# One VectorE tile fewer in a split-softmax attention kernel, with the order planned for a shorter ScalarE wave

## The chip, the cores and the metric

The kernel runs on one core of a Trainium2 chip. The metric is the device time of one execution in microseconds (us), the median of several runs; each profiled execution also has a span, some 2 us shorter, from its first to its last instruction. Every run carries a state; only fast runs are compared. The engines are PE (TensorE matmul; PEld is its weight load), ACT (ScalarE), DVE (VectorE), POOL (GpSimd) and SP, which here only issues transfers (SPq in the trace).

## The reference

```python
B, H, S, D = 1, 32, 2048, 640     # Dh = 20
qn = q / (sqrt((q * q).sum(-1, keepdims=True)) + eps)
kn = k / (sqrt((k * k).sum(-1, keepdims=True)) + eps)
logits = einsum('bhqd,bhkd->bhqk', qn, kn) * t[None, :, None, None]
attn = softmax(logits, axis=-1)
return einsum('bhqk,bhkd->bhqd', attn, v)
```

There are 32 heads of 2048 x 2048 logits with only 20 channels, so the exponentials are the work: 134 million of them.

## The kernel before

Each head's keys form 16 row blocks. For each block and each of four groups of 512 queries TensorE writes one unit (128 x 512) of logits to PSUM. Then one of two engines does the exponential. ScalarE takes waves of 2 and 3 units in turn, from PSUM tile psA to p_ring:

```python
act[w] = add("ACT", f"exp{w}", lambda e, tk: e.activation(
    p_ring[...], psA[...], ACT.Exp), 0.0633 + n / 1200.0, qks + war, w)
```

VectorE takes tiles of 4 units. It turns a logit into the bits of an fp16 power of two (two pieces per tile, psD to xt) and makes three shifted copies (ss), whose weighted sum with xt corrects the approximation. For some tiles the third copy is made by GpSimd instead:

```python
e.tensor_scalar(xt[...], psD[...], X_MUL, X_ADD, ALU.mult, ALU.add)   # VectorE, 2 per tile
e.tensor_scalar(dst, x, float(PHASES[i]), None, ALU.add)              # VectorE, 2 or 3 per tile
e.tensor_tensor(dst..bitcast(I32), xt..bitcast(I32), two, ALU.add)    # GpSimd, the third of some tiles
```

How many of the 16 blocks of each head go to VectorE is the list DVE_TILES; for how many of these GpSimd makes the third copy is KDN. Everything is written as tasks with a planned duration. A planner in the kernel's own source simulates the engines, picks an order for each, and the program is emitted in that order; the engines then run their lists strictly in order and meet at semaphores. The planned durations therefore never change an instruction, only where it stands. An unused branch, with accumulating transfers, leaves one instruction behind in the kernel before:

```python
z_cst = memset("POOL", cst[:, :], PHASES[2], 0.3, -70)   # 128 x 2048 int16, read by nobody
```

Of the kernel before, what the change touches and what calls it, by code (L numbers as in the profile page):

```python
# [13 lines left out]
I16 = mybir.dt.int16  # L14
# [7 lines left out]
PHASES = (256, 512, 768)  # L22
# [21 lines left out]
class Program:  # L44
# [2 lines left out]

    SEM_LAT = {"PE": 0.20, "ACT": 0.17, "DVE": 0.14, "POOL": 0.15, "SP": 0.0}

    SWITCH = 0.5  # L50
    LIGHT = 9.0
    TICK = 3.41
    LOAD = 3500.0
# [3 lines left out]
    PE_REST = 4.2  # L57
    PV_SLACK = 0.6
    OVER = 0.03
    SPARE = 0.0  # L60
    DSL = 0.6
    HOLDA = 0.7
    HPE = 0.1
    HDV = 0.08
    HOLD = {"DVE": HDV, "PE": HPE}

    def __init__(self):
# [3 lines left out]
    def add(self, eng, name, fn, dur, deps=(), pri=0.0, lat=0.0, dma=None):  # L71
        t = Task(eng, name, fn, dur, deps, pri, lat, dma)
        self.tasks.append(t)
        return t

    def schedule(self):
# [4 lines left out]
        for k in range(self.PASSES):  # L81
# [28 lines left out]
            for j, t in enumerate(pe):  # L110
                for tier in range(4):
                    m = j - 1
                    while lo[j] and loads[j] < self.LOAD and m >= lo[j]:
                        u = pe[m]
                        if u.modes and u not in heavy and u not in more:
                            cost = u.modes[1][2] - u.dur
                            if tier == 3 or cost <= 0 or tier == 1 and cost <= min(
                                    v.start for v in u.users) - u.end - 0.2 - self.SPARE or tier == 2 and u.name[2] == "A":
                                more.add(u)
# [12 lines left out]
    def list_schedule(self):  # L132
# [80 lines left out]
        while events or ready["POOL"]:  # L213
# [13 lines left out]
            for e in touched:  # L227
# [5 lines left out]
                if e in soon:  # L233
                    held = [r for r in ready[e] if r[2].name[:2] not in ("t1", "tr") and
                            not (e == "PE" and r[2].name[0] == "q" and (
                                r[2].name[2] != "A" or free["ACT"] - now - r[2].dur * 2 - 0.35 < self.HOLDA)) and hold(e, now, r[2].dur)]
                    if len(held) == len(ready[e]):
# [4 lines left out]
                if e == "PE":  # L242
                    if self.DSL is not None and any(r[2].name[0] == "q" for r in ready[e]):
                        more = sum(r[2].dur for r in ready["DVE"]) + self.DSL
                        x = min((r for r in ready[e] if r[2].name[0] == "q"), key=lambda r: (
                            (free["ACT"] if r[2].name[2] == "A" else free["DVE"] + more) - r[2].dur, r[0], r[1]))
                    else:
                        x = min(ready[e], key=lambda r: (r[0] + (0.0 if r[2].name[:2] == last_pe[0] else self.SWITCH), r[1]))
                    ready[e].remove(x)
# [93 lines left out]
def bass_standalone__qk_norm__prompt_kernel(  # L343
# [7 lines left out]
    B, H, S, D = q.shape  # L351
# [23 lines left out]
    PE_MM = 0.23  # L375
    MORE = 12
    DLM = 2
    DVE_TILES = [4, 4, 4, 5, 5, 5, 5, 5, 4, 5, 5, 5, 5, 4, 5, 5, 5, 5, 5, 5, 4, 5, 5, 5, 5, 6, 5, 5, 5, 4, 4, 6]
    NDMAX = 6
    NPOOL, FPOOL = True, True  # L380
    SQPOOL = False
    RSPOOL = False
    TTRATE = 0.00168
    TTDUR, TTWIN = 0.8, 0.55
    NCH = 1
    KDN = (4, 5, 2, 4, 3, 2, 4, 4, 2, 2, 4, 3, 3, 3, 4, 2, 4, 3, 3, 4, 3, 3, 5, 2, 3, 5, 2, 4, 2, 3, 3, 2)
    ADUR, ALAT = 0.95, 6.5
    PSH = 2
    ASTEP, AOFF = 2, 0
    ACCN = (0, 0, 0, 0, 0, 0, 0, 0, 0, 0, 0, 0, 0, 0, 0, 0, 0, 0, 0, 0, 0, 0, 0, 0, 0, 0, 0, 0, 0, 0, 0, 0)  # L390
    NLAST = 1
    PCH, PRATE = 512, 0.00164
    SHP = 0.0

    with ExitStack() as es:  # L395
        sbuf = lambda name, shape, dt: es.enter_context(nc.sbuf_tensor(name, shape, dt))
# [4 lines left out]
        act_scr = sbuf("act_scr", [128, 32], F32)  # L401
        ones = sbuf("ones", [128, 512], BF16)
        two = sbuf("two", [128, 1], I32)
        cst = sbuf("cst", [128, 2048], I16)
        ident = sbuf("ident", [128, 128], BF16)
        qk_sb = [sbuf(f"qk_sb{i}", [128, 2 * R, D], BF16) for i in range(NB)]
        vaug = [sbuf(f"vaug{i}", [128, R, 32], BF16) for i in range(NV)]
# [9 lines left out]
        xt = [sbuf(f"xt{i}", [128, GD * 2048], I16) for i in range(NX)]  # L417
# [10 lines left out]
        add = prog.add  # L428
# [4 lines left out]
        def memset(eng, ap, val, dur, pri):  # L433
            return add(eng, "z", lambda e, tk: e.memset(ap, val), dur, pri=pri)
# [20 lines left out]
        while not waves or waves[-1][-1] < NA - 1:  # L455
            i = waves[-1][-1] + 1 if waves else 0
# [11 lines left out]
        ld_t = dma("SP", "ld_t", tb16[:, :], bass.AP(t.tensor, 0, [[0, 128], [1, H]]), [], -40, "t")  # L468
        z_one = memset("DVE", ones[:, :], 1.0, 0.2, -99)
        memset("POOL", two[:, :].bitcast(I16), PHASES[PSH], 0.1, -98)  # L470
        z_cst = memset("POOL", cst[:, :], PHASES[2], 0.3, -70)
        z_id = add("POOL", "id", lambda e, tk: e.affine_select(
            ident[:, :], ones[:, 0:128], [[1, 128]], ALU.is_equal, 0.0, base=0, channel_multiplier=-1), 0.5, [z_one], -99)
        z_kx = memset("DVE", kx[:, :].rearrange("p (r w) -> p r w", w=32)[:, :, D:32], 0.0, 0.5, -97)
# [280 lines left out]
        def add_wave(w):  # L755
            us = waves[w]
            slot = w % 2
            hs = sorted({A_units[i][0] for i in us})
            pair = next(([i, i + 1] for i in range(len(us) - 1)
                                          if A_units[us[i]][2] // 2 != A_units[us[i + 1]][2] // 2), [])  # L760
            parts = pair + [i for i in range(len(us)) if i not in pair]

            def f_qk(eng, rows):
                last = None
                for i in parts:
                    h, r, g = A_units[us[i]]
                    last = qk_mm(eng, h, r, g, psA[:, (slot * WAVES[0] + i) * 512:(slot * WAVES[0] + i + 1) * 512], rows)
                return last
            deps = [act.get(w - 2)]
            for h in hs:  # L770
                deps += qk_deps([A_units[u] for u in us if A_units[u][0] == h])
            qk = add("PE", f"q3A{w}", lambda e, tk: f_qk(e, tk.rows), PE_MM, deps, w - 10000.0)
            if len(us) == 3 and LIGHT3:
                qk.modes = [("q3", 32, PE_MM + 0.01, 384.0), ("q2", 64, PE_MM * 2, 768.0)]
            elif len(us) == 3:
                qk.modes = [("q2", 64, PE_MM * 2, 768.0), ("qk", 128, PE_MM * 3, 1536.0)]
            else:
                qk.modes = [("q2", 64, PE_MM, 256.0 * len(us)), ("qk", 128, PE_MM * len(us), 512.0 * len(us))]
            qks = [qk]
            for h in hs:  # L780
                qk_users[h] += qks
            p0 = us[0] % NP
            n = len(us) * 512
            war = [pv_of_group[(u - NP) // 4] for u in us if u >= NP]
            act[w] = add("ACT", f"exp{w}", lambda e, tk: e.activation(  # L785
                p_ring[:, p0 * 512:p0 * 512 + n], psA[:, slot * WAVES[0] * 512:slot * WAVES[0] * 512 + n], ACT.Exp),
                0.0633 + n / 1200.0, qks + war, w)

        def add_group(i):
            us = list(range(4 * i, 4 * i + 4))  # L790
# [10 lines left out]
        dusers = {}  # L801

        def add_dgroup(jg):
            js = D_groups[jg]
            sx, se = jg % NX, jg % NE
            w = 2048 * len(js)
            old = lambda n, ring: dusers.get((n, jg - ring), [])
            t1s = []
            for i, j in enumerate(js):
                h, rg = D_tiles[j]  # L810
                due = h + (j - d0[h] + 0.3) / DVE_TILES[h] - DLEAD
# [23 lines left out]
            x = xt[sx][:, 0:w]  # L835
# [3 lines left out]
            sh = []  # L839
            h0, n0 = D_tiles[js[0]][0], js[0] - d0[D_tiles[js[0]][0]]  # L840
            nd0 = DVE_TILES[h0]
            order = [(n * ASTEP + AOFF) % nd0 if math.gcd(ASTEP, nd0) == 1 else n for n in range(nd0)]
            kind = order.index(n0)
            by_dma = jg >= 2 and h0 < H - NLAST and kind < ACCN[h0]
            by_pool = jg >= 2 and not by_dma and kind < ACCN[h0] + KDN[h0]
            for i in range(len(PHASES)):
                dst, war = ss[i][se], t1s + old(f"s{i}", NE)
                if i == 2 and by_dma:
                    sh.append(None)
                elif i != PSH or not by_pool:  # L850
                    sh.append([dv(f"s{i}.", lambda e, tk, i=i, dst=dst: e.tensor_scalar(  # L851
                        dst[:, 0:w], x, float(PHASES[i]), None, ALU.add), 0.533, war)])
                else:
                    sh.append([])
                    for c in range(0, w // 2, PCH):
                        n = min(PCH, w // 2 - c)
                        u = add("POOL", f"s{i}.{js[0]}.{c}", lambda e, tk, i=i, dst=dst, c=c, n=n: e.tensor_tensor(  # L857
                            dst[:, 2 * c:2 * (c + n)].bitcast(I32), xt[sx][:, 2 * c:2 * (c + n)].bitcast(I32),
                            bass.AP(two, 0, [two[:, :].ap[0], [0, n]]), ALU.add), 0.25 + n * PRATE, war, due + SHP)
                        u.win = 0.02 + n * PRATE  # L860
                        sh[-1].append(u)
            dusers["x", jg] = [u for us in sh if us for u in us]
            parts = [("x", xt[sx], t1s, None)] + [(f"s{i}", ss[i][se], sh[i], i) for i in range(len(PHASES))]
            for nm, tile, dep, ph in parts:
                us = dusers.setdefault((nm, jg), [])
                if dep is None:
                    us = dusers["x", jg]
                    tile = xt[sx]
                    dep = [add("POOL", f"acc{js[0]}", lambda e, tk: e.dma_start(x, cst[:, 0:w], accum_op=ALU.add), ADUR,
                               us + [z_cst], due + 0.1, lat=ALAT, dma=f"A{sx}")]  # L870
                for i, j in enumerate(js):
                    h, rg = D_tiles[j]
                    p = add("PE", f"pv{nm}{j}", lambda e, tk, h=h, rg=rg, i=i, tile=tile, ph=ph: pv_mm(
                        e, h, lambda g: rg[g],
                        lambda g: tile[:, 2048 * i + 512 * GORD[g]:2048 * i + 512 * GORD[g] + 512].bitcast(FP16), ph),
                        PE_MM, dep + pv_base(h) + (vsc[h] if ph is not None else []), due + 0.2)
                    pv_users[h].append(p)
                    us.append(p)
# [76 lines left out]
```

## Time and profile before

| | before |
|---|---|
| median time, us | 665.11 (3 runs, 664.69 to 666.1) |
| span of the profiled run, us | 662.8 |
| ACT busy, DVE busy, POOL busy | 99%, 99%, 56% |
| ScalarE waves | 573, holding 1432 units |
| VectorE tiles / shifts on VectorE / on GpSimd | 154 / 363 / 99 |

The profile's main rows stand in the prediction below. One more view: ScalarE's time line, with start, length and, in brackets, the idle time before a row. Idle time occurs twice, both before 55 us:

```profile
9.39 21.36 ACT L785 ACTIVATE p_ring<-psA 128x1024 bf16<-128x1024 f32 x19
31.58 22.75 ACT L785 ACTIVATE p_ring<-psA 128x1536 bf16<-128x1536 f32 x20 [0.83 <-PE psA L694]
54.99 603.63 ACT L785 ACTIVATE p_ring<-psA 128x1536 bf16<-128x1536 f32 x534 [0.66 <-PE psA L694]
```

I count waves from 0, so the two waits stand before waves 19 and 39.

### The profile page before, as it was taken

To read this page: it belongs to the slowest core of one execution; us is meant where nothing else is said; L and a number is where in the kernel's file an instruction comes from. 1 tells how busy PE (TensorE), PEld (TensorE's weight loads), DVE (VectorE), ACT (ScalarE), POOL (GpSimd) and SP (SyncE) were. 2 spreads that over 40 slices of the span, in tenths; PEclk is the share of its full clock that TensorE was granted. 3 is DMA by queue.
4 is the path that set the end of the run, shared out by engine and by line. 5 is a ranking of instruction groups with operands and counts; after the bars stand their busy time and mean duration, and the time that the engine had idled before them with its cause. 6 is when DMAs were issued, how large, how long until landed. Compare 5 with 4: busy or idle time off the path is not lost.

```text
span 662.8 us, 14627 instructions
## 1 busy us (share of the span) xinstructions
PE 579.4 (87%) x5949; PEld 163.2 (25%) x5971; DVE 655.2 (99%) x927; ACT 655.1 (99%) x582; POOL 369.7 (56%) x375
## 2 busy tenths in 40 slices
PE   7787989988898888898889898888989889988997
PEld 2222222222222222222222222222222222222222
DVE  9999999999999999999999999999999999999997
ACT  8999999999999999999999999999999999999997
POOL 3346565565654456655666556565675664554550
PEclk9999999999999999999999999999999999999999
DMA  5454524243242432513435250353514224032200
GB/s 64 64 80 81 66 43 80 30 74 48 53 75 31 82 35 59 70 20 84 43 73 65 48 80 10 75 62 65 67 28 79 37 53 73 3 77 35 54 7 11
DMA packets 196723, 36.24 MB, mean 55 GB/s; under 512 B 172592, under 2 KB 196656, under 8 KB 196656
## 3 DMA queue, kind: packets, MB, share of 16 engines
q1 hardware_dynamic: 196512, 35.22, 34.0%
q8 instruction: 47, 0.77, 0.5%
q14 instruction: 20, 0.16, 0.1%
q10 hardware_dynamic: 144, 0.08, 0.1%
HBM read 7.87 MB, written 2.62 MB: 16 GB/s over the span
## 4 chain that ended last, share of the span: by engine, by line
ACT 91%; DVE 6%; DMA 1%; issue 1%; PE 0%; SPq 0%; ACTq 0%
ACT p_ring L785 91%; DVE xt L831 3%; DVE ss L851 1%; DMA qkT<-qkn 1%; DVE rs_sum L556 0%; DMA qk_sb<-in_k_dram 0%; DVE rs_u L559 0%; DMA qz<-qkT 0%; DVE sq L554 0%; SPq L431 0%; DVE qz L665 0%; DVE oT L727 0%; ACTq L395 0%; DVE kx L673 0%; DVE o_stage L738 0%
## 5 line engine op out<-in xcount | busy, mean ns | idle before, releaser
L785 ACT ACTIVATE p_ring<-psA 128x1024 bf16<-128x1024 f32 (+1 forms) x573 | 647.7, 1402 | 1.5 <-PE psA L694 1.5
L831 DVE TENSOR_SCALAR xt<-psD 128x1024 int16<-128x1024 f32 x308 | 374.9, 1217 | 1.7 <-PE psD L694 0.7
L857 POOL TENSOR_TENSOR ss<-xt,two 128x512 int32<-128x512 int32 x198 | 250.8, 1267 | 171.6 <-DVE ss L851 79.5
L694 PE MATMUL psA<-qz,kR 32*128 32x512 bf16 (+2 forms) x1063 | 217.5, 385 | 47.0 <-ACT p_ring L785 42.4
L851 DVE TENSOR_SCALAR ss<-xt 128x2048 int16<-128x2048 int16 x363 | 243.2, 688 | 0.0
L714 PE MATMUL psO<-ss,vph 128*32 128x512 f16 x1848 | 171.2, 385 | 0.7 <-POOL ss L857 0.7
L714 PE MATMUL psO<-p_ring,vaug 128*32 128x512 bf16 x1432 | 132.2, 385 | 0.7 <-ACT p_ring L785 0.7
L694 PE MATMUL psA<-qz,qkT 32*128 32x512 bf16 (+2 forms) x354 | 115.4, 384 | 15.0 <-ACT p_ring L785 13.4
L694 PE MATMUL psD<-qz,kR 64*128 64x512 bf16 (+1 forms) x456 | 118.5, 385 | 9.5 <-DVE xt L831 6.5
L694 PEld LDWEIGHTS psA<-qz,kR 32*128 32x128 bf16 (+2 forms) x1074 | 52.9, 92 | 183.1 <-ACT p_ring L785 179.7
L522 POOL TENSOR_SCALAR vph<-vaug 128x160 f16<-128x160 bf16 (+2 forms) x96 | 37.1, 386 | 48.9 <-DVE ss L851 22.5
L589 POOL TENSOR_TENSOR qkn<-qk_sb,rs_r 128x640 bf16<-128x640 bf16 x29 | 47.8, 1647 | 28.0 <-DVE ss L851 13.6
L714 PEld LDWEIGHTS psO<-ss,vph 128*32 128x32 f16 x1848 | 44.4, 94 | 73.1 <-issue 56.1
L694 PE MATMUL psD<-qz,qkT 64*128 64x512 bf16 (+1 forms) x153 | 57.6, 385 | 3.8 <-DVE xt L831 3.3
L714 PE MATMUL psO<-xt,vaug 128*32 128x512 f16 x616 | 59.9, 384 | 0.0
L714 PEld LDWEIGHTS psO<-p_ring,vaug 128*32 128x32 bf16 x1432 | 35.0, 94 | 54.9 <-issue 46.0
L738 POOL TENSOR_TENSOR o_stage<-oT,rec 128x320 bf16<-128x320 f32 x30 | 29.3, 978 | 33.3 <-DVE rec L730 15.8
L694 PEld LDWEIGHTS psD<-qz,kR 64*128 64x128 bf16 (+1 forms) x462 | 28.9, 93 | 71.5 <-DVE xt L831 57.2
L694 PEld LDWEIGHTS psA<-qz,qkT 64*128 64x128 bf16 (+2 forms) x358 | 28.0, 92 | 61.7 <-ACT p_ring L785 59.6
L556 DVE TENSOR_REDUCE rs_sum<-sq 128x32 f32<-128x640 bf16 x32 | 26.0, 812 | 0.1
L727 DVE STREAM_TRANSPOSE oT<-psO 128x512 f32<-128x512 f32 x32 | 22.7, 709 | 2.0 <-PE psO L714 2.0
L714 PEld LDWEIGHTS psO<-xt,vaug 128*32 128x32 bf16 x616 | 15.9, 94 | 23.1 <-issue 19.2
(47 smaller groups left out, 92.0 us busy)
## 6 DMA issues: line engine op xcount, KB each, us to landing
kR<-qkT SPq DMA_DIRECT2D x62, 96.0 KB, 2.2
qz<-qkT SPq DMA_DIRECT2D x124, 32.0 KB, 1.8
kR<-qkT SPq DMA_DIRECT2D x62, 64.0 KB, 2.0
qk_sb<-in_k_dram SPq DMA_DIRECT2D x32, 80.0 KB, 2.5
vaug<-in_v_dram SPq DMA_DIRECT2D x32, 80.0 KB, 3.6
qk_sb<-in_q_dram SPq DMA_DIRECT2D x124, 20.0 KB, 2.6
out_dram<-o_stage SPq DMA_DIRECT2D x31, 80.0 KB, 2.3
kR<-qkT SPq DMA_DIRECT2D x62, 32.0 KB, 1.9
```

The source lines that it names most:

```text
L522: vsc[h] = [add("POOL", f"vs{h}", lambda e, tk, i=i: e.tensor_scalar(vph[bv][:, i, 0:nd, :], vaug[bv][:, R - nd:R, :], 2.0 ** (-PHASES[i] ...
L556: sums.append(dv("sum", lambda e, tk, i=i, sqb=sqb: e.tensor_reduce(rs["sum"][:, 2 * R * i:2 * R * (i + 1)], sqb[:, :, :], AXIS_X, ALU.add ...
L589: u = add("POOL", f"norm{h}", lambda e, tk, x=x, b=b, i=i, j=j: e.tensor_tensor(qkn[b][:, j:j + m, 0:D], x[:, j:j + m, :], bc(rs["r"][:, 2 ...
L694: return eng.matmul(dst, lhsT, mov, tile_position=(p0, 0))
L714: last = eng.matmul(psO[32 * g:32 * g + 32, :], w, rhs_of(g), start=start, stop=False, skip_group_check=True, tile_position=(0, 32 * g))
L727: trO[h] = add("DVE", f"tr{h}", lambda e, tk: e.transpose(oT[:, :, :].rearrange("p r d -> p (r d)"), psO[:, :]), 0.63, [lambda: pv_users[h ...
L738: fin[h] = add("POOL" if pool else "DVE", f"fin{h}", lambda e, tk: e.tensor_tensor(st, src, rb, ALU.mult), TTDUR if pool else 0.40, [rc] + ...
L785: act[w] = add("ACT", f"exp{w}", lambda e, tk: e.activation(p_ring[:, p0 * 512:p0 * 512 + n], psA[:, slot * WAVES[0] * 512:slot * WAVES[0] ...
L831: t1_prev[nchunk[0]] = add("DVE", f"t1.{j}.{k}", lambda e, tk, o=o, slot=slot: e.tensor_scalar(xt[sx][:, o:o + W1], psD[:, slot * W1:slot ...
L851: sh.append([dv(f"s{i}.", lambda e, tk, i=i, dst=dst: e.tensor_scalar(dst[:, 0:w], x, float(PHASES[i]), None, ALU.add), 0.533, war)])
L857: u = add("POOL", f"s{i}.{js[0]}.{c}", lambda e, tk, i=i, dst=dst, c=c, n=n: e.tensor_tensor(dst[:, 2 * c:2 * (c + n)].bitcast(I32), xt[sx ...
```

## The change

Its intent: a trace seemed to say that the fixed part of a ScalarE wave is 0.051 us rather than 0.0633. If so, ScalarE has room, one tile can move to it from VectorE, and the order should be planned with the new figure. The other constants and lists were chosen anew for that.

```diff
-    SWITCH = 0.5
+    SWITCH = 0.1
...
-    SPARE = 0.0
-    DSL = 0.6
-    HOLDA = 0.7
+    SPARE = 0.05
+    DSL = 0.0
+    HOLDA = 0.6
...
-    HDV = 0.08
+    HDV = 0.04
...
-    DVE_TILES = [4, 4, 4, 5, 5, 5, 5, ... 5, 6, 5, 5, 5, 4, 4, 6]
+    DVE_TILES = [4, 4, 4, 5, 5, 4, 5, ... 5, 6, 4, 5, 5, 4, 5, 6]
...
+    EXP0 = 0.051
...
-    KDN = (4, 5, 2, 4, 3, 2, ... 2, 4, 2, 3, 3, 2)
+    KDN = (5, 5, 2, 4, 3, 2, ... 2, 4, 3, 3, 1, 4)
...
-        z_cst = memset("POOL", cst[:, :], PHASES[2], 0.3, -70)
...
-                0.0633 + n / 1200.0, qks + war, w)
+                EXP0 + n / 1200.0, qks + war, w)
...      (and the unused branch around the accumulating transfers goes)
```

More of the change, by code (lines that the diff above doesn't have):

```diff
@@ L377, in bass_standalone__qk_norm__prompt_kernel @@
     DLM = 2
-    DVE_TILES = [4, 4, 4, 5, 5, 5, 5, 5, 4, 5, 5, 5, 5, 4, 5, 5, 5, 5, 5, 5, 4, 5, 5, 5, 5, 6, 5, 5, 5, 4, 4, 6]
+    DVE_TILES = [4, 4, 4, 5, 5, 4, 5, 5, 4, 5, 5, 5, 5, 4, 5, 5, 5, 5, 5, 5, 4, 5, 5, 5, 5, 6, 4, 5, 5, 4, 5, 6]
     NDMAX = 6
@@ L385, in bass_standalone__qk_norm__prompt_kernel @@
     NCH = 1
-    KDN = (4, 5, 2, 4, 3, 2, 4, 4, 2, 2, 4, 3, 3, 3, 4, 2, 4, 3, 3, 4, 3, 3, 5, 2, 3, 5, 2, 4, 2, 3, 3, 2)
-    ADUR, ALAT = 0.95, 6.5
+    KDN = (5, 5, 2, 4, 3, 2, 4, 4, 2, 1, 3, 3, 4, 3, 4, 2, 4, 2, 3, 4, 3, 3, 5, 2, 3, 5, 2, 4, 3, 3, 1, 4)
     PSH = 2
     ASTEP, AOFF = 2, 0
-    ACCN = (0, 0, 0, 0, 0, 0, 0, 0, 0, 0, 0, 0, 0, 0, 0, 0, 0, 0, 0, 0, 0, 0, 0, 0, 0, 0, 0, 0, 0, 0, 0, 0)
-    NLAST = 1
     PCH, PRATE = 512, 0.00164
@@ L403, in bass_standalone__qk_norm__prompt_kernel @@
         two = sbuf("two", [128, 1], I32)
-        cst = sbuf("cst", [128, 2048], I16)
         ident = sbuf("ident", [128, 128], BF16)
@@ L843, in add_dgroup @@
             kind = order.index(n0)
-            by_dma = jg >= 2 and h0 < H - NLAST and kind < ACCN[h0]
-            by_pool = jg >= 2 and not by_dma and kind < ACCN[h0] + KDN[h0]
+            by_pool = jg >= 2 and kind < KDN[h0]
             for i in range(len(PHASES)):
                 dst, war = ss[i][se], t1s + old(f"s{i}", NE)
-                if i == 2 and by_dma:
-                    sh.append(None)
-                elif i != PSH or not by_pool:
+                if i != PSH or not by_pool:
                     sh.append([dv(f"s{i}.", lambda e, tk, i=i, dst=dst: e.tensor_scalar(
@@ L861, in add_dgroup @@
                         sh[-1].append(u)
-            dusers["x", jg] = [u for us in sh if us for u in us]
+            dusers["x", jg] = [u for us in sh for u in us]
             parts = [("x", xt[sx], t1s, None)] + [(f"s{i}", ss[i][se], sh[i], i) for i in range(len(PHASES))]
@@ L865, in add_dgroup @@
                 us = dusers.setdefault((nm, jg), [])
-                if dep is None:
-                    us = dusers["x", jg]
-                    tile = xt[sx]
-                    dep = [add("POOL", f"acc{js[0]}", lambda e, tk: e.dma_start(x, cst[:, 0:w], accum_op=ALU.add), ADUR,
-                               us + [z_cst], due + 0.1, lat=ALAT, dma=f"A{sx}")]
                 for i, j in enumerate(js):
```

## The prediction

> **What bounds the kernel now.** I read the busy shares first, then the chain that ended last, then the costliest groups, then stretches of time, and last single instructions of ScalarE. The busy shares name two candidates:
>
> ```profile
> PE 579.4 (87%) x5949; PEld 163.2 (25%) x5971; DVE 655.2 (99%) x927; ACT 655.1 (99%) x582; POOL 369.7 (56%) x375
> ```
>
> VectorE (DVE) and ScalarE (ACT) are both at 99%, because the kernel splits one job between them: a softmax exponential is done either by a ScalarE wave (PSUM to p_ring) or by VectorE (PSUM to xt, then three integer shifts, some of them on GpSimd). In the middle of the kernel neither rests; in this table by stretches the columns are PE, PEld, DVE, ACT, POOL:
>
> ```profile
> 60.00:160.00 100.00, 89.63 (x943) 25.32 (x948) 99.82 (x138) 100.00 (x89) 58.26 (x60) 1.00 0.39 61
> 260.00:360.00 100.00, 88.48 (x923) 24.64 (x927) 99.94 (x141) 100.00 (x89) 60.95 (x58) 1.00 0.38 60
> ```
>
> Which of the two sets the end is told by the chain in order of time (start, length, what):
>
> ```profile
> 54.18 0.05 issue
> 54.23 0.39 PE psD L694 x2
> 54.62 0.35 PE psA L694 x3
> 54.97 0.02 issue
> 54.99 602.71 ACT p_ring L785 x533
> 657.70 0.93 ACTq L395
> 658.63 0.04 issue
> 658.67 0.43 PE psO L714 x4
> 659.10 0.02 issue
> 659.12 0.73 DVE oT L727
> ```
>
> From 55 us to the tail it is ScalarE alone, 533 waves with no link to anybody else. So what counts is the time per wave. Waves hold 2 and 3 units of 512 columns in turn. The 533 waves start and end with a three-unit one, so 267 x 3 + 266 x 2 = 1333 units. At 512/1200 us a unit (the slope in the kernel's own plan) that is 568.7 us; the rest, 34.0 us over 533 waves, is **0.0637 us a wave**, nearly the 0.0633 with which the order of the kernel before was planned.
>
> The change says that the trace has 0.051 instead, so I looked at single waves. Three answers of the timeline, each one instruction longer than the last and all from the same start:
>
> ```profile
> 298.78 1.76 ACT L785 ACTIVATE p_ring<-psA 128x1536 bf16<-128x1536 f32 x1
> 298.78 2.68 ACT L785 ACTIVATE p_ring<-psA 128x1536 bf16<-128x1536 f32 x2
> 298.78 4.02 ACT L785 ACTIVATE p_ring<-psA 128x1536 bf16<-128x1536 f32 x3
> ```
>
> From end to end, two units take 2.68 - 1.76 = 0.92 us and three take 4.02 - 2.68 = 1.34. Less 0.853 and 1.280 that leaves 0.06 each, 0.063 on the mean of the pair. Going through all recorded waves one by one, I find ends 1.343 to 1.345 and 0.915 to 0.917 us apart almost without exception, while starts are commonly 1.330 and 0.903 apart, which is 0.050 over the columns. A start thus runs ahead of the end before it, from 0.10 up to 0.42 us, and then falls back; the ends do not notice. So 0.051 is the distance of starts. Throughput is the distance of ends: 0.063.
>
> The other rows that I price with:
>
> ```profile
> L785 ACT ACTIVATE p_ring<-psA 128x1024 bf16<-128x1024 f32 (+1 forms) x573 | 647.7, 1402 | 1.5 <-PE psA L694 1.5
> L831 DVE TENSOR_SCALAR xt<-psD 128x1024 int16<-128x1024 f32 x308 | 374.9, 1217 | 1.7 <-PE psD L694 0.7
> L857 POOL TENSOR_TENSOR ss<-xt,two 128x512 int32<-128x512 int32 x198 | 250.8, 1267 | 171.6 <-DVE ss L851 79.5
> L851 DVE TENSOR_SCALAR ss<-xt 128x2048 int16<-128x2048 int16 x363 | 243.2, 688 | 0.0
> ```
>
> A mean is longer than the cost here, since neighbours overlap: in the chain an xt piece takes 1.13 us and a shift 0.60. ScalarE's whole idle is 1.5 us, two waits before 55 us.
>
> **What the Trainium skill says.** "ScalarE: Activation LUTs", section What ACT_TABLE_LOAD costs: an ACTIVATE with immediate scale and bias takes 186 ns + 0.833 ns per column, and neighbours overlap by about 93 ns, which would leave 93 ns a wave. The trace agrees on the slope; its shortest wave is 1.018 us at 1024 columns, 165 ns over 853; and the fixed part that remains is 63 ns, less than the page gives and more than the change assumes. "Perfetto Trace Analysis", section Identifying the Most-Contended Engine, takes occupancy as a fair measure for Vector and Scalar: here it gives a tie at 99%, and only the chain breaks it. "SBUF — State Buffer", section Who interferes with whom: VectorE in a two-port mode and GpSimd block each other for a whole instruction. The trace shows GpSimd waiting for VectorE's shifts (79.5 us in the L857 row), which bears on where shifts are placed. "TensorE: Matmul & The Clock Gate", Part 1, ties the clock to activity in windows of about 3.4 us; the trace grants 1.00 in all stretches.
>
> **The change part by part.** (1) Tiles. The list sums to 154 before and 153 after: heads 5 and 26 lose one, head 30 gains one. A tile is 4 units. Before, (32 x 16 - 154) x 4 = 1432 units go to ScalarE in 573 waves; after, 1436 in 575, the last of one unit. ScalarE gains 4 x 0.4267 = 1.71 us for columns and 2 x 0.063 = 0.13 for waves: **+1.83 us, all on the chain**.
> (2) VectorE loses two xt pieces, 2 x 1.13 = 2.26 us. The number of tiles whose third shift goes to GpSimd, counted with the kernel's own rule, falls from 99 to 98, so VectorE's shifts go from 462 - 99 = 363 to 459 - 98 = 361: 2 x 0.60 = 1.20. Together **-3.5 us**, beside a busy ScalarE, so not on the chain. GpSimd loses 2 x 1.27 = 2.5 us, TensorE 12 PV matmuls of 3896; neither is the bound.
> (3) The planned cost of a wave, 0.0633 to 0.051, and the other planning constants (kind switch, hold times, slack): no instruction gets faster. Only the order within engines changes. The plan now believes ScalarE needs 575 x 0.0123 = 7.1 us less than it does. I think that this is why a tile went its way: in the planner's books ScalarE's load falls by 7.1 - 1.8 = 5.3 us and VectorE's by 3.5, so both seem to finish some 3.5 us earlier.
> (4) The removed accumulate-by-DMA branch was unused (its counts are all zero). With it goes one 1.8 us GpSimd memset at the start, where the chain runs through the first load, VectorE and the transposes, not through GpSimd. Worth nothing.
>
> Sum: ScalarE starts its first wave at 9.4 us, and 4.2 us of the span lie after its last wave (658.6 to 662.8); I expect both to stay. Its waits were 1.5 us. With the waits unchanged, 662.8 + 1.8 = 664.6 us of span, and as the median time was 2.3 us over the span, **about 666.9; I say 667.0**. With no waits at all it is about 665.3.
>
> **Rivals.** *The 0.051 is right.* If starts were the pace, VectorE's relief and the shorter waves would both be real and the time would fall by about 3.5 us to 661.6. For it: starts do come 0.050 apart for stretches. Against it: over 533 linked waves the mean is 0.0637, and a wave that starts 0.42 us early ends no sooner. I give it 5%.
> *The order fits worse and ScalarE waits.* Each engine runs its list in order, TensorE too. If the plan thinks a wave is done 12 ns too soon, TensorE reaches the refill of psA early and waits there; that delays psD and VectorE, which now has 3.5 + 1.8 us to spare, rather than ScalarE. So drift should fall on VectorE. But places where the plan itself leaves ScalarE waiting may be worse, and the first 60 us are laid out with new constants: 1 to 3 us, hence up to 669 or 670.
> *The relief removes waits.* The two waits before 55 us end with TensorE; one lies behind the transfer of qz, the other behind psD of VectorE. Heads 0 to 4 keep their tiles, so I expect little: at best 1.5 us back, about 665.3.
> *The clock drops* because TensorE's work is spread thinner than planned (by 1%): nothing near it in the trace, but it would add microseconds.
> *VectorE collides more with GpSimd:* it has over 5 us to lose before that shows in the time.
>
> **Range and chances.** The centre is the chain plus 1.83. Below it lie 1.5 us of removable waits and a small chance that the pace is the starts'; above it lie new waits. So 665.2 to 669.6. Two per cent is 13.3 us, far more than any of these: faster 0.01, same 0.975, slower 0.015.
>
> **What will show it.** Right if p_ring has 575 waves with ends still 1.344 and 0.916 apart and busy about 649.5 us; if the chain is ScalarE for some 600 us; if VectorE's xt count is 306 and shifts 361, with more than 3 us of new idle or stretched time on VectorE; and if ScalarE's idle is 1 to 4 us. Wrong if ends come 1.331 and 0.904 apart, if the first wave starts well before 9.4 us, if the chain goes through VectorE for long stretches in the middle (VectorE bound by a worse order), or if the clock falls below 1.00.

## The result, and the profile after

The changed kernel took 666.21 us (median of 4 runs, 665.47 to 666.35), the kernel before 665.61 beside it (4 runs). The ratio is 1.0004, with a 95% interval from 0.9982 to 1.0026. Ratios here and below are the mean time of one kernel's fast runs over that of the other's fast runs of the same rounds, so they are not quite the ratios of the quoted medians. Repeated with more runs (E9 below): 665.43 against 665.12, ratio 1.0001, interval 0.9988 to 1.0014. So the time is the same, and if anything a few tenths of a microsecond longer.

The busy shares of the kernel after, and the rows to hold against those in the prediction:

```profile
PE 582.0 (88%) x5931; PEld 162.7 (25%) x5959; DVE 652.7 (98%) x923; ACT 656.9 (99%) x584; POOL 369.6 (56%) x372
...
L781 ACT ACTIVATE p_ring<-psA 128x1024 bf16<-128x1024 f32 (+1 forms) x575 | 649.7, 1414 | 1.4 <-PE psA L690 1.2
L827 DVE TENSOR_SCALAR xt<-psD 128x1024 int16<-128x1024 f32 x306 | 373.0, 1219 | 5.3 <-PE psD L690 3.3
L850 POOL TENSOR_TENSOR ss<-xt,two 128x512 int32<-128x512 int32 x196 | 251.0, 1280 | 173.4 <-DVE ss L844 76.4
...
L844 DVE TENSOR_SCALAR ss<-xt 128x2048 int16<-128x2048 int16 x361 | 240.8, 684 | 0.2
```

ScalarE is 2.0 us busier in its waves (647.7 to 649.7). VectorE has fewer instructions, and its idle time before xt pieces grew from 1.7 to 5.3 us: the relief turned into waiting. The chain is still ScalarE's:

```profile
70.02 589.05 ACT p_ring L781 x521
659.07 0.50 ACTq L393
659.57 0.04 issue
659.61 0.43 PE psO L710 x4
```

ScalarE's time line after shows an earlier start, and a longer first wait:

```profile
8.43 21.36 ACT L781 ACTIVATE p_ring<-psA 128x1024 bf16<-128x1024 f32 x19
30.99 628.57 ACT L781 ACTIVATE p_ring<-psA 128x1536 bf16<-128x1536 f32 x556 [1.20 <-PE psA L690]
```

The start is 0.96 us earlier, which I had not expected. In this one execution TensorE's clock also fell to half for 3.4 us at 33 us (mean granted clock 0.97 from 10 to 60 us); in the profile of the repeat it was 1.00 throughout.

The kernel before ran 30 times beside the experiments. Its 19 runs with a granted clock of 0.998 or more took 664.2 to 665.1 us, its 11 runs below that 664.7 to 668.5. Which of the two causes the other is not shown. If one keeps to runs at 0.998 or more in the rounds of E9 (a choice made after the fact), the changed kernel takes 665.39 us on the mean of 4 and the kernel before 664.67 on the mean of 6: the change then costs some 0.7 us.

Because ScalarE works without a break from about wave 60 on, its recorded ends make an exact ledger. It is read out of the trace wave by wave for seven profiled runs, and it carries most of what follows (us from the span's start):

| kernel | wave 0 starts | wave 19 starts | wave 60 ends | last wave ends | wave 60 to last |
|---|---|---|---|---|---|
| before | 9.39 | 31.58 | 79.98 | 658.62 | 578.64 |
| E2, before without the memset | 8.42 | 31.00 | 79.36 | 658.30 | 578.94 |
| E12, before with 22 more reciprocals | 9.36 | 30.58 | 79.17 | 657.78 | 578.61 |
| after | 8.43 | 30.99 | 79.17 | 659.56 | 580.39 |
| E9, after again | 8.42 | 30.93 | 78.84 | 659.23 | 580.39 |
| E10, after with the memset back | 9.39 | 30.63 | 78.77 | 659.16 | 580.39 |
| E11, after with 22 more reciprocals | 8.44 | 30.40 | 78.25 | 658.65 | 580.39 |

E2's last figure contains one stop of 0.38 us, at wave 279.

### The profile page after: what moved, and what is told of

It is laid out like the page before. It is cut to its first block, busy times and chain, and to the rows that moved or that the text cites. A ratio compares the mean times of both kernels' runs of the same rounds, so it can differ in the third digit from the quotient of the medians.

```text
span 663.7 us, 14584 instructions
## 1 busy us (share of the span) xinstructions
PE 582.0 (88%) x5931; PEld 162.7 (25%) x5959; DVE 652.7 (98%) x923; ACT 656.9 (99%) x584; POOL 369.6 (56%) x372
## 4 chain that ended last, share of the span: by engine, by line
ACT 91%; DVE 6%; PE 1%; DMA 1%; issue 0%; SPq 0%; ACTq 0%
ACT p_ring L781 90%; DVE xt L827 3%; DVE ss L844 1%; DMA qkT<-qkn 1%; ACT qz L474 0%; PE psA L690 0%; DVE rs_sum L552 0%; PE psD L690 0%; DVE oT L723 0%; PE psO L710 0%; DMA qz<-qkT 0%; SPq L428 0%; DVE o_stage L734 0%; ACT L464 0%; ACT qz L658 0%
## 5 line engine op out<-in xcount | busy, mean ns | idle before, releaser
L781 ACT ACTIVATE p_ring<-psA 128x1024 bf16<-128x1024 f32 (+1 forms) x575 | 649.7, 1414 | 1.4 <-PE psA L690 1.2
L710 PE MATMUL psO<-ss,vph 128*32 128x512 f16 x1836 | 163.1, 385 | 0.0
L690 PE MATMUL psA<-qz,qkT 32*128 32x512 bf16 (+2 forms) x353 | 117.3, 388 | 16.8 <-ACT p_ring L781 15.4
L710 PE MATMUL psO<-p_ring,vaug 128*32 128x512 bf16 x1436 | 129.6, 385 | 0.2 <-ACT p_ring L781 0.2
L518 POOL TENSOR_SCALAR vph<-vaug 128x160 f16<-128x160 bf16 (+2 forms) x96 | 39.7, 414 | 48.6 <-DMA vaug<-in_v_dram 22.8
L710 PEld LDWEIGHTS psO<-ss,vph 128*32 128x32 f16 x1836 | 41.7, 94 | 71.8 <-issue 56.2
L690 PEld LDWEIGHTS psA<-qz,qkT 32*128 32x128 bf16 (+2 forms) x359 | 28.6, 92 | 63.2 <-ACT p_ring L781 61.8
```

The lines of the kernel that those rows point to most:

```text
L518: vsc[h] = [add("POOL", f"vs{h}", lambda e, tk, i=i: e.tensor_scalar(vph[bv][:, i, 0:nd, :], vaug[bv][:, R - nd:R, :], 2.0 ** (-PHASES[i] ...
L690: return eng.matmul(dst, lhsT, mov, tile_position=(p0, 0))
L710: last = eng.matmul(psO[32 * g:32 * g + 32, :], w, rhs_of(g), start=start, stop=False, skip_group_check=True, tile_position=(0, 32 * g))
L781: act[w] = add("ACT", f"exp{w}", lambda e, tk: e.activation(p_ring[:, p0 * 512:p0 * 512 + n], psA[:, slot * WAVES[0] * 512:slot * WAVES[0] ...
```

## The experiments

The edits are shown shortened.

My theory after the result: ScalarE's throughput is the bound; its fixed cost is 0.063 us; the added 1.83 us are on the path; the removed memset gives back the 0.96 us; VectorE's relief is spare. The main rival: VectorE is still a bound, or the order itself decides. It turned out that parts of both are true.

**E3: is the fixed part 0.063 or 0.051?** Waves of three units are issued as two instructions in the changed kernel, order untouched.

```diff
-e.activation(p_ring[... n], psA[... n], ACT.Exp)
+for x, y in ((0, 1024), (1024, 1536)) if n == 1536 else ((0, n),):
+    e.activation(p_ring[... x:y], psA[... x:y], ACT.Exp)
```

> The changed kernel with each wave of three units issued as two instructions (1024 and 512 columns), 287 more ScalarE instructions over the same columns; planned order untouched. If the fixed part is 0.063 us (distance of ends): ScalarE busy and span +18.1 us, time about 684.3. If it is 0.051 (distance of starts): +14.6 us, about 680.8. If ScalarE did not set the pace: clearly less than 14.

Measured: 683.44 us, 1.0276 of before; the span is 681.8 us, 18.1 over the changed kernel's first profile. The row of waves (instructions, busy, mean) has 287 more instructions and 18.1 us more busy time than the row after:

```profile
L784 ACT ACTIVATE p_ring<-psA 128x1024 bf16<-128x1024 f32 (+1 forms) x862 | 667.8, 1110 | 1.4 <-PE psA L690 1.2
```

18.1 / 287 = 0.0631. The second half of a split wave waits for nobody, so this is the engine's own cost. The figure 0.051 is excluded by 3.5 us.

**E1, E2, E10: what is the memset worth?** In the trace of before, GpSimd's memset of cst runs across VectorE's first small operation of head 0 (start, length):

```profile
4.02 1.82 POOL L434 MEMSET cst<- 128x2048 int16 x1
```

```profile
4.50 1.38 DVE L559 TENSOR_SCALAR rs_u<-rs_sum 128x32 int32<-128x32 int32 x1
```

The memset ends at 5.84 and the small operation at 5.88. After, with no memset, the same operation takes 0.18 us:

```profile
4.64 0.18 DVE L555 TENSOR_SCALAR rs_u<-rs_sum 128x32 int32<-128x32 int32 x1
```

E1 and E10 are the same kernel, the changed one with the memset put back.

```diff
+        cst = sbuf("cst", [128, 2048], I16)
+        z_cst = memset("POOL", cst[:, :], PHASES[2], 0.3, -70)
```

> The changed kernel with the one GpSimd memset of cst put back; every other instruction in the same order. Theory A (the memset holds up VectorE's first small shift-type op of head 0, as the trace of before shows 1.38 us for it against 0.18 after): that op takes about 1.4 us again, the first ScalarE wave starts at 9.4 us instead of 8.4, span +0.9 to +1.0 us, time about 667.2. Rival B (the start moved for the new order's sake, or by chance of the loads): first wave stays at 8.4 to 8.6 us and the time at 666.2.

> The changed kernel with the unused memset put back, again, because its profile fell in the slow state before. If the memset costs what the start shows: first wave 9.4 us instead of 8.4, span and time 0.6 to 1.0 us above the changed kernel's in the same rounds. Rival (the wait of ScalarE near 31 us takes it back): first wave 9.4 us but that wait shorter by the same amount, time equal.

E2 takes it out of the kernel before:

```diff
-        z_cst = memset("POOL", cst[:, :], PHASES[2], 0.3, -70)
```

> The kernel before with only the unused memset of cst (and the unused branch) taken out; the rest in the same order. Theory A: first ScalarE wave at 8.4 us instead of 9.4, and as the chain is ScalarE from there, span 661.8 to 662.1 and a time about 0.95 us below before, some 664.6, which would beat both kernels. Rival B: no change, 665.6. A third outcome: the gain is swallowed by the two waits of ScalarE before 55 us, which would then be longer by about 0.9 us in all.

In all three the emitted order of all other instructions is identical to the parent's. The start of wave 0 follows the memset exactly: about 9.4 us with it (E1 9.40, E10 9.39), 8.4 without (E2 8.42). But the time does not follow. E2: 664.82 us, 0.9999 of before (0.9985 to 1.0013). E1: 665.62, 1.0012 (0.9996 to 1.0028). E10: 665.70 against 665.43 for E9 in the same rounds, with profiled spans of 663.3 and 663.4. The time line of E10 shows where the microsecond went:

```profile
9.39 60.08 ACT L783 ACTIVATE p_ring<-psA 128x1024 bf16<-128x1024 f32 x53
69.62 589.54 ACT L783 ACTIVATE p_ring<-psA 128x1536 bf16<-128x1536 f32 x522 [0.15 <-PE psA L692]
```

Started late, ScalarE does not wait before wave 19 at all; started early, it waits 1.2 us. Wave 19 needs the second head's transposed operands. That transposition is one entry in SP's list, and SP reaches it after some 13 us of issuing one transfer after another, whether head 0 was early or not. From 10 us on SP's list in the kernel before and in the one after:

```profile
10.01 3.92 SPq L675 DMA_TRANSPOSE kR<-kx  x3
13.98 2.12 SPq L431 DMA_DIRECT2D vaug<-in_v_dram  x2
...
23.80 1.36 SPq L607 DMA_TRANSPOSE qkT<-qkn  x1
```

```profile
9.95 3.94 SPq L671 DMA_TRANSPOSE kR<-kx  x3
13.93 2.02 SPq L428 DMA_DIRECT2D vaug<-in_v_dram  x2
...
23.32 1.36 SPq L603 DMA_TRANSPOSE qkT<-qkn  x1
```

In E10, with the memset, it comes at 23.08. Over the seven traces of the ledger it comes at 22.88 to 23.80, and wave 19 starts 7.5 to 7.8 us after it in each. What it transposes (qkn) was ready by 20.6 us in each, so it waited for SP's list and not for VectorE. So the rival of E10's expectation holds: the early start is real, and no run shows it to be worth anything (at a granted clock of 0.998 or more, E2 is 0.3 us longer than before, and E10 0.1 us longer than E9). Wave 19 starts anywhere from 30.40 to 31.58 us in the ledger, and that does not sort by memset.

**E4, E5: is VectorE's relief free? First try.** Six useless shifts more, in heads 5, 9, 13, 17, 21 and 25, in the changed kernel and in the one before.

```diff
+if ex is not None: e.tensor_scalar(ex[:, 0:w], x, float(PHASES[i]), None, ALU.add)
 return e.tensor_scalar(dst[:, 0:w], x, float(PHASES[i]), None, ALU.add)
```

> The changed kernel with six useless VectorE shifts more (one in each of heads 5, 9, 13, 17, 21, 25, written to spare tiles), 6 x 0.60 = 3.6 us of VectorE work; order otherwise untouched. Theory: VectorE has over 3 us to spare since it lost a tile, ScalarE is the pace, so the time moves by less than 1 us (666.2 to 667.2). Rival (VectorE is still a pace-setter, both at 98 to 99 per cent): +3.6 us, about 669.8.

> The kernel before with the same six useless VectorE shifts, 3.6 us of VectorE work. Theory: before, VectorE and ScalarE were nearly balanced, VectorE having at most some 2 us to spare, so the time rises by 1 to 3.6 us, more than in the changed kernel. Rival (ScalarE alone was the bound before as well): less than 1 us, as in the changed kernel.

Measured: 671.31 us for the changed kernel (1.0096 of before) and 669.74 for before (1.0072). Both slow down by more than the 3.6 us put in, so my expectation failed. The trace of E4 shows that the test cost more than I had priced:

```profile
117.35 0.68 DVE L849 TENSOR_SCALAR extra<-xt 128x2048 int16<-128x2048 int16 x1
117.51 1.42 POOL L856 TENSOR_TENSOR ss<-xt,two 128x512 int32<-128x512 int32 x1 [0.35 <-DVE rs_r L568]
117.95 1.53 DVE L850 TENSOR_SCALAR ss<-xt 128x2048 int16<-128x2048 int16 x1
119.40 1.21 DVE L828 TENSOR_SCALAR xt<-psD 128x1024 int16<-128x1024 f32 x1
```

The GpSimd addition had been placed so that it would run beside an xt piece. The extra shift took its place, and the next shift then waited for GpSimd: 1.53 us instead of 0.68. That happened right behind four of the six extra shifts (three in E5), so the sum is nearer 3.6 + 4 x 0.85 = 7.0 us, in lumps. By the recorded ends of its waves E4 lost 6.0 us after wave 60. The collision is not the whole cause: of the two extra shifts without one, the shift at 195 us still made ScalarE 0.97 us late in the waves behind it, the one at 444 us only 0.13. I needed smaller work that collides with nobody.

**E11, E12: second try.** Each reciprocal of heads 5 to 26 is done twice: 22 pieces that add 0.16 us each between recorded ends.

```diff
+if 5 <= h < 27: e.reciprocal(extra[h - 5][:, :], oT[:, :, D])
 return e.reciprocal(rec[:, :], oT[:, :, D])
```

> The changed kernel with each reciprocal of heads 5 to 26 done twice: 22 x 0.16 = 3.5 us of VectorE work in small pieces, instead of six large ones, and of a kind that is no shift. If VectorE's relief of 3.5 us is there to be used but only a little at a time (ScalarE being 1 per cent slower than planned lets VectorE regain about 0.1 us in 10 us): less than 1 us slower than the changed kernel. If VectorE can regain nothing: 3.5 us or more slower.

> The kernel before with the same 22 reciprocals more, 3.5 us of VectorE work in small pieces. Planned with the true 0.063 us, ScalarE runs as planned, so VectorE can regain time only where its own list has room: 1 to 3.5 us slower than before, more than in the changed kernel. If the small pieces are absorbed here too, VectorE had room before the change as well.

Measured: 664.90 us for the changed kernel and 664.81 for the one before; both ratios to before are 0.9992, with intervals that hold 1. In the ledger, wave 60 to the last takes 580.39 us in E11, the very figure of the kernel without the extra work, and 578.61 in E12 against 578.64. E12's last row of ScalarE's time line, from wave 39 on, can be held against the third row under "Time and profile before":

```profile
54.17 603.60 ACT L791 ACTIVATE p_ring<-psA 128x1536 bf16<-128x1536 f32 x534 [0.66 <-PE psA L695]
```

So 3.5 us of VectorE work cost nothing in **either** kernel. My idea that the two engines were balanced before is wrong as well: VectorE had that room already, at 99% busy; 3.5 us is half a per cent of the span. Where the room hides can be read from VectorE's recorded ends. Taking 1.132 us as the usual distance of an xt piece from the operation before it, the pieces overran it by 5.5 us in sum before, by 11.8 after, by 8.9 in E11 and by 2.9 in E12. Most of the added work thus went into that stretch; an instruction that has started and waits counts as busy.

**E6, E7, E8: the parts of the change one by one.** E6 is the changed kernel with the old two lists; E7 the kernel before with the new two lists; E8 the changed kernel with the old planned cost.

```diff
 E6:  DVE_TILES, KDN  as before       (new constants kept)
 E7:  DVE_TILES, KDN  as after        (old constants kept)
 E8: -EXP0 = 0.051   +EXP0 = 0.0633
```

> The changed kernel's planning constants, with the tile list and GpSimd counts of before (154 VectorE tiles, 573 waves). Theory: ScalarE has 1.83 us less to do and starts at 8.4 us; if VectorE keeps up, span about 661.9 and time about 664.4; if the order planned with 0.051 puts VectorE's extra tile on the path, up to 666.5. Rival (the tile move is what pays for the early start's loss): slower than the changed kernel.

> The kernel before with only the new tile list and GpSimd counts; memset and old planning constants (0.0633) kept. Theory: first wave at 9.4 us, ScalarE +1.83 us, time about 667.4 (before plus 1.8), with VectorE's relief unused. Rival (VectorE's relief is on the path): 662 to 664.

> The changed kernel with only the planned fixed part of a wave set back to 0.0633. Theory: the planned figure changes the order but no instruction; ends stay 1.344 and 0.916 us apart, time within 1 us of the changed kernel (665.2 to 667.2). Whether the TensorE clock still dips for 3.4 us at 33 us, which could cost some 0.4 us, is open. Rival (0.051 fits better and the order gains by it): slower by 1 us or more.

Measured: 672.26, 713.84 and 711.32 us; 1.0118, 1.0743 and 1.0706 of before. All three miss what I expected, two of them by over 40 us. The largest single stop in E8 shows what happened there. ScalarE, VectorE and SP near 570 us:

```profile
592.57 2.37 ACT L781 ACTIVATE p_ring<-psA 128x1536 bf16<-128x1536 f32 x2 [19.67 <-PE psO L710]
```

```profile
573.90 3.77 SPq L428 DMA_DIRECT2D kR<-qkT  x6
577.71 1.81 SPq L428 DMA_DIRECT2D vaug<-in_v_dram  x2
579.57 1.40 SPq L428 DMA_DIRECT2D qk_sb<-in_k_dram  x1
581.01 2.68 SPq L428 DMA_DIRECT2D qk_sb<-in_q_dram  x4
...
585.62 1.14 DVE L550 TENSOR_TENSOR sq<-qk_sb 128x640 bf16<-128x640 bf16 x1 [15.28 <-DMA qk_sb<-in_q_dram]
```

VectorE's next list entry was the square of a later head, whose q had not been loaded, because that load stood in SP's list behind two transpositions. Those had been held until 560 us by GpSimd's normalisation (16.0 us is the longest such wait there), and between them and the load came over 20 other transfers. VectorE, TensorE and ScalarE all stood still, for 14 to 20 us, behind one late load. The clock's dip to half for 20.5 us begins at 573.0 us, after VectorE had run out of work at 570.3: it follows the stop and doesn't cause it.

Nor did the waits arise only on the chip. Asked for the waits in its own plan, the kernel's planner has most of them already:

```
planned by the kernel's own planner, us (a plan, not a measurement), and the measured end
              last ScalarE wave ends   planned ScalarE idle   longest planned idle   measured end
before         655.1                    0.0                    none                   658.6
after          650.3                    0.4                    0.3                    659.6
E6             656.7                    8.6                    2.6                    664.1
E7             705.7                   48.8                   22.9                    706.3
E8             700.9                   43.9                   20.9                    696.6
```

The plan's four longest gaps in E6 (2.61, 1.88, 1.16 and 0.92 us) were 2.57, 1.41, 1.15 and 0.93 us on the chip. ScalarE's whole idle between waves on the chip was 6.9, 45.5 and 35.9 us in E6, E7 and E8. So a pair of lists belongs to one set of constants; each of the three other pairings that I ran left holes, two of them of tens of microseconds. E6, E7 and E8 therefore do not measure what the tile or the constant is worth; they measure an order that nobody had tuned. What the table does show is what the change promised: it planned to end ScalarE 4.8 us sooner, and ended it 0.9 us later. The plan was short by 9.3 us, of which 575 x 0.0123 = 7.1 us is the mis-set cost of a wave, and the rest start and waits.

**E9: the changed kernel again.**

> The changed kernel itself, again, beside the others on one chip. Account by the recorded ends of its waves: start 8.4, work 649.1, lateness about 1.9, tail 4.2, span 663.7 and time about 666; if the first result was typical, a ratio to before of 1.000 to 1.003.

Its numbers are given above: the same again, the ledger's last column equal to 0.01 us.

I also let the planner try some 4,000 random variations of the two lists with 0.0633 and the memset gone. None planned shorter than the lists of before, so there was no better version to run. That search is no proof that there is none.

## Why the prediction was right or wrong

**The range and the verdict** were right: 666.2 and 665.4 us lie in the range 665.2 to 669.6, though 0.8 and 1.6 us under the 667.0 that I named. About 0.5 us of that is the anchor: I put 2.3 us between span and time, a median of three runs less the span of a fourth. That fourth, the profiled one, took 664.62 us over a span of 662.8, so 1.8. The rest is in the early waits, below.

Two of my own signs of being wrong did appear: the first wave started well before 9.4 us (8.43), and the clock fell below 1.00 (0.97 from 10 to 60 us in the first profile). The chain is ScalarE's all the same, so I had taken the wrong things for signs.

**Step 1, 0.063 us a wave and not 0.051,** was right. E3 measured 0.0631.

**Step 2, +1.83 us on the chain,** was right to the hundredth where ScalarE runs unbroken: 580.39 against 578.64 us from wave 60 to the last. Before had one wait of 0.08 us in that stretch, so 580.39 - 578.56 = 1.83.

**"ScalarE starts its first wave at 9.4 us ... I expect both to stay" and "Worth nothing" of the memset.** The first failed: the start moved to 8.4. My reason, that the chain goes through VectorE and not through GpSimd, missed that GpSimd can hold VectorE up; I had named that very lock, but looked for it only among the shifts. (The 79.5 us that I set beside it are no sign of it either: the planner makes each third copy wait for a chosen VectorE operation, by semaphore.) The second came true for another reason than mine, which is luck: the early start runs into the wait for the second head.

**"Its waits were 1.5 us. With the waits unchanged"** is the term that was mis-sized. Up to the end of wave 60 the three profiles with the old order took 79.98, 79.36 and 79.17 us and the four with the new one 79.17, 78.84, 78.77 and 78.25. The means, 79.50 and 78.76, differ by 0.7 us. A part of it is plain: the wait before wave 39, 0.77 us in all three profiles of the old order, is not there in the new one, which has smaller ones instead. That offsets under half of the 1.83. Whether the new order or VectorE's relief took that wait away is not separated, and the two sets of profiles touch (79.17 in both). On the means of the ledger's last wave ends, 659.15 against 658.23, the change then costs 0.9 us, and 0.7 among runs at a granted clock of 0.998 or more. The medians say 0.3 to 0.6, with an interval of about 0.9 us on either side in the repeat, which holds all of these.

**VectorE's relief, -3.5 us off the chain,** was right, and stronger than I argued: even before the change 3.5 us were to spare (E12). "It has over 5 us to lose" is too simple, though: small pieces were absorbed, larger ones were mostly not, with a GpSimd collision or without (E4, E5).

**The rival "the order fits worse: 1 to 3 us"** did not come true for the tuned pair (ScalarE's idle was 1.4 us, against 1.5 before) and was far too small for the parts taken alone: 8 to 49 us over the kernel before. **"The clock drops: nothing near it in the trace"** was too confident. It dropped for 3.4 us in one profile, and for over 20 us at a time in E7 and E8; the runs of one kernel at the lower granted clock are also the longer ones, as said above.

What stays open: why SP's issuing up to the second head's transposition takes up to 0.9 us longer in one run than in another, why runs at a lower granted clock are longer, and what one tile would be worth under an order tuned as long for it as these two were.

## What to carry to other kernels

Take an engine's cost per instruction from the distance between ends while it runs unbroken, not between starts: starts can run ahead and mean nothing. A busy share of 99% doesn't prove a bound; add a little harmless work to that engine and see. And where a planner sets the order, a wrong duration can make you move work the wrong way: here a tile went to the one engine that had no room, for 1.83 us where that engine runs unbroken.

## What the Trainium skill lacked or had wrong

- "ScalarE: Activation LUTs", What ACT_TABLE_LOAD costs: 186 ns fixed less about 93 ns of overlap leaves 93 ns a wave, as an estimate. Here, from PSUM to SBUF, it is 63 ns between ends (E3: 18.1 us over 287 instructions). The overlap is no constant either: a wave's recorded start mostly lies 0.10 to 0.42 us before the end of the wave before, with no effect on the ends.
- "Perfetto Trace Analysis", Identifying the Most-Contended Engine, calls occupancy a fair measure for Vector. VectorE stood at 99% in the kernel before and took 3.5 us more work at no cost (E12): half a per cent of its time, most of it time in which an instruction that had started was waiting.
- "SBUF — State Buffer", Who interferes with whom, has the lock right: VectorE's operation ended 0.04 us after GpSimd's memset (1.38 us instead of 0.18). What a reader needs beside it is that even a memset nobody reads does this, and that a lump of VectorE work can shift the collision to the next shift (1.53 instead of 0.68 us).
